# Scores of two pairs of heads issued as one run in every second step of a window attention

## The chip, the cores and the metric

The kernel runs on one core of a Trainium2 chip. The metric is the device time of one execution in microseconds, the median of several. Before the change three runs gave 798.02, 800.39 and 802.64 us; the median is 800.39 us.

A core has a matrix engine (TensorE, PE in the profile; its weight loads are listed as PEld), a vector engine (VectorE, DVE), a scalar engine (ScalarE, ACT) and GpSimd (POOL). Each works through its own queue in order; they wait for each other through semaphores. SyncE (SP) issues DMAs. TensorE writes to PSUM, which VectorE and ScalarE read.

## The reference

An attention over a window of 128 keys and 4 "sink" keys, then a Fourier mixing and a feed-forward network, in float32, for 4 batches of 768 positions, 8 heads of 64:

```python
scores = scale * np.matmul(q, k.transpose(0, 1, 3, 2))
keep = is_sink | in_window
scores = np.where(keep, scores, -1000000000.0)
a = np.exp(scores - np.max(scores, axis=-1, keepdims=True))
a = a / (np.sum(a, axis=-1, keepdims=True) + 1e-09)
x = np.matmul(a, v)                      # then heads side by side: (4, 768, 512)
u = x + np.real(np.fft.fft(np.fft.fft(x, axis=1), axis=2))
un = (u - mu) / np.sqrt(var + 1e-06)     # over the last axis
out = u + np.maximum(un @ w_ch1, 0.0) @ w_ch2
```

## The kernel before

**Blocks and steps.** The 768 positions of a batch are 6 blocks of 128 queries, so there are 24 blocks, numbered g. The 8 heads are 4 pairs, numbered hp. One *step* s is one pair of heads of one block: s = 4 g + hp, 96 steps in all, and k = s mod 4. A block needs its own 128 keys, the 128 of the block before it and the 4 sink keys.

**What is done for a pair** (names as they stand in the profile's rows):

- scores, on TensorE: queries times keys into a PSUM tile s. The queries and keys are split into a high and a low part (qs, and two rings of key blocks, ring), and three products of each head are added, so a pair is six matmuls (L723, 64 rows of the array each). The first block of a batch needs only its own keys, unsplit: two matmuls (L717). There are two PSUM tiles s, used in turn: the scores of step s can start when the softmax sums of step s - 2 have read theirs.
- merge, on VectorE (L730): the scores of the older keys are copied over those of the newer where the window wants them.
- soft1, on VectorE (L742): two instructions, one for each head, add the mask, take the extremum into mx and write to sm in SBUF.
- expo, on ScalarE (L748): the exponentials and their sums.
- For two pairs together: trans_p on TensorE (pt, L773, four transposes), copy_p on ScalarE (pta, L780), newer_p and older_p on GpSimd (ptl L789, pta L797, which separate newer from older keys), av on TensorE (xt, L811: the values, 128x64 pieces of the array).
- sink_p on GpSimd (sk, L759 and L760) and, once in a block, trans_sink on TensorE (pk, L829) and copy_sink on ScalarE (skt, L834). pk and pt use one and the same PSUM buffer.
- Once in a block: copy_x on ScalarE (xs, L816), turn_x on TensorE (x, L823 and L825), inverse on VectorE (L764, L765) and store_x on VectorE (L839: the product of x and 1/sum into u or us).
- Once in a block the next block's queries and keys are split: q_hi and k_hi on ScalarE (L686, L695), q_lo on VectorE or GpSimd (L691), k_lo on VectorE (L700, into ring).

**What sets the order.** The attention's instructions are recorded in the order of the text, with no scheduler, up to step 97 (`CUT`). In a step first the DMAs and the scores are recorded, then for each engine a list from `SCHEDULE[s >= 36][engine][k]`: names of the work above, and numbers and letters ("A", 0 to 3, "V", "G", "T") that stand for other events put at that step. `STEP_LAG` says how many steps after its scores a piece of a pair comes, `BLOCK_AT` the same for work done once in a block. With `lag(scores, s, 0)` step s records its own scores; with "merge" and "soft1" at a lag of 1, VectorE's list of step s holds the merge and sums of step s - 1.

**Fourier events.** Once four blocks of a batch are stored, the Fourier mixing of that batch is laid over the following steps: folds on VectorE and GpSimd (L351 to L367), then in TensorE's "T" events a first stage (za, zb, zr, L394) and a second one (a, b, dc, L421 and L442), whose results ScalarE and VectorE take out of PSUM (L399 to L409, L425 to L448). They use one PSUM bank of their own and at times the buffer of x.

**After step 97** a scheduler orders what is left: the tail of the last batches' Fourier work, the conversion of the FFN's weights on VectorE (cv, cw, L590 to L592), and the FFN of the first of seven groups. From the second group on the FFN is in the order of the text again; it is some 500 us of matmuls (h, L617, and o, L1147).

The lines that the change and the steps of the prediction touch are `STEP_LAG` (L71), the lists "V" of `SCHEDULE`, and `lag(scores, s, 0)` (L1000).

Of the kernel before, what the change touches and what calls it, by code (L numbers as in the profile page):

```python
# [67 lines left out]
POOL_LO = (1, 2, 3), ()  # L68
PHASE = 36

STEP_LAG = {"merge": 1, "soft1": 1, "expo": 2, "sink_p": 2, "trans_p": 3, "copy_p": 4, "newer_p": 5, "older_p": 5, "av": 7}  # L71
BLOCK_AT = {
    "copy_x": 11,
    "copy_sink": 8,
# [24 lines left out]
            ["copy_x", "A", "copy_p", "copy_sink", "expo", "q_hi", "k_hi", "mid_hi", "sink_hi"],  # L99
        ],  # L100
        "V": [
            ["merge", "inverse", "store_x", "q_lo", "k_lo", "sink_lo", "V", "soft1", 3, 0, "mid_lo", 1, 2],
            [3, "merge", 1, "V", "mid_lo", "soft1", "inverse", "store_x", "q_lo", "k_lo", 0, "sink_lo", 2],
            ["sink_lo", 0, "merge", 3, 1, "V", 2, "soft1", "store_x", "inverse", "k_lo", "mid_lo", "q_lo"],
            ["merge", "inverse", 0, "soft1", "k_lo", "V", 3, "store_x", "q_lo", "mid_lo", "sink_lo", 2, 1],
        ],
        "G": [
            ["q_lo_g", "mid_lo_g", "newer_p", "G", "older_p", "k_lo_g", "sink_p"],
# [16 lines left out]
            ["expo", "copy_x", "copy_p", "copy_sink", "A", "q_hi", "k_hi", "mid_hi", "sink_hi"],  # L125
        ],
        "V": [
            ["merge", "inverse", "store_x", "q_lo", "k_lo", "sink_lo", "soft1", 3, 1, 0, "V", 2, "mid_lo"],
            [2, "merge", 0, "sink_lo", 3, 1, "V", "soft1", "inverse", "q_lo", "store_x", "mid_lo", "k_lo"],
            ["sink_lo", "q_lo", 0, "merge", "soft1", 3, "V", 2, 1, "store_x", "inverse", "k_lo", "mid_lo"],  # L130
            ["merge", 1, "inverse", 3, 2, "soft1", "store_x", "q_lo", "V", 0, "k_lo", "mid_lo", "sink_lo"],
        ],
        "G": [
            ["q_lo_g", "mid_lo_g", "newer_p", "k_lo_g", "G", "older_p", "sink_p"],
# [81 lines left out]
def kernel(  # L216
# [15 lines left out]
    V, A, G, T = nc.vector, nc.scalar, nc.gpsimd, nc.tensor  # L232
# [37 lines left out]
    def run(general):  # L270
        tag = "g" if general else ""
        with ExitStack() as p1:
# [11 lines left out]
            def run_ev(s, eng):  # L284
                for fn in ev.pop((s, eng), ()):
                    fn()
# [346 lines left out]
            def window_attention(fourier, load_constants):  # L633
                with ExitStack() as pa:
# [207 lines left out]
                    def lag(fn, s, d):  # L842
                        if 0 <= s - d < len(steps):
                            fn(*steps[s - d])

                    last = len(steps) + 14
                    with ExitStack() as man:
# [131 lines left out]
                        s = 0  # L979
                        extra.append(lambda name: ps_t.tile([P, 512], F32, tag="x", name=name)  # L980
                                     if s % NP in X_AT and not X_NOT[0] <= s <= X_NOT[1] and s < len(steps) - 2 else None)
                        while s < last:
# [14 lines left out]
                                if g % NB == 2:  # L997
                                    load_v(kb(g) + 1)
                            run_ev(s, "S")
                            lag(scores, s, 0)  # L1000
                            if s == 0:
                                for (a, b, e), hi, lo in ((K0_AT, lambda: k_hi(kb(0)), lambda: k_lo(kb(0), V)),
                                                          (Q1_AT, lambda: q_hi(1), lambda: q_lo(1, V)),
# [365 lines left out]
```

## Time and profile before

| | us |
|---|---|
| median of 3 runs | 800.39 |
| the profiled execution | 802.72 |
| its span, first to last instruction | 800.9 |
| TensorE busy in it (95%) | 764.3 |
| VectorE busy (60%) | 479.8 |
| ScalarE busy (33%) | 263.2 |
| GpSimd busy (26%) | 205.1 |

The span and the busy times are of one profiled execution, 2.3 us above the median. A row of the timeline reads: start and length in us, engine, line, operation, output<-inputs, the part of the array (128\*64: rows by columns) and the shape, how many instructions are merged into it (x6), and in brackets how long the engine stood idle before it and what ended that. Matmuls are pipelined: one of them takes about 0.3 us from start to end, but the next starts long before that, so the place that a piece holds on TensorE is read from its start to the next piece's start. A row of busy time by stretch reads: the stretch, its length, then for each engine the us it was busy and (x) its instructions, the granted clock of TensorE (1.00 is full speed), the share of the DMA engines and GB/s.

### The profile page before, as it was taken

The page shows a single profiled execution, that of the slowest core. Times are in us where ns is not written, and L with a number is a line of the kernel's source. Part 1 is how long each engine was busy: PE and PEld are TensorE (multiplying, and loading weights), DVE is VectorE, ACT ScalarE, POOL GpSimd, SP SyncE. Part 2 cuts the span into 40 slices and gives each one's busy share as a digit, 9 for nine tenths or more (in the row PEclk, how much of TensorE's full clock was granted, in tenths as well). Part 3 has the DMA queues.
Part 4 walks back from the last instruction along what each step waited for, and adds up shares of the span by engine and source line. Part 5 has one row for each costly group of instructions (what it writes and reads, how often), then busy time and mean ns, then how long its engine had stood idle before and what let it go on. Part 6 is the DMA issues. An engine that isn't in the chain of part 4 may idle for free.

```text
span 800.9 us, 12364 instructions
## 1 busy us (share of the span) xinstructions
PE 764.3 (95%) x4539; PEld 631.8 (79%) x4539; DVE 479.8 (60%) x1387; ACT 263.2 (33%) x752; POOL 205.1 (26%) x298
## 2 busy tenths in 40 slices
PE   7988997998999899999999999999999999999995
PEld 5766886876778788889888888888888888888895
DVE  7989579899899679853256714663356515511211
ACT  6887586676642223312111111111111110110110
POOL 3568479579673335500000000000000000000000
PEclk9997999999999899999999999999999999999998
DMA  8652331324523446420010002000200001000100
GB/s 291 232 169 70 122 122 55 111 68 148 162 78 105 132 134 204 136 106 1 12 42 1 1 0 106 1 1 0 79 1 0 1 1 52 1 1 0 53 1 32
DMA packets 19926, 56.73 MB, mean 71 GB/s; under 512 B 2412, under 2 KB 2540, under 8 KB 19472
## 3 DMA queue, kind: packets, MB, share of 16 engines
q1 hardware_dynamic: 19568, 52.09, 19.6%
q0 software_dynamic: 288, 3.76, 1.1%
q8 instruction: 38, 0.62, 0.3%
q14 instruction: 32, 0.26, 0.1%
HBM read 46.39 MB, written 9.45 MB: 70 GB/s over the span
## 4 chain that ended last, share of the span: by engine, by line
PE 81%; DVE 11%; ACT 3%; issue 2%; POOL 1%; DMA 1%; SPq 0%; ACTq 0%; POOLq 0%; DVEq 0%
PE o L1147 32%; PE h L617 32%; PE xt L811 5%; PE s L723 3%; PE pt L773 2%; PE za L394 2%; DVE cv L591 1%; DVE sm L742 1%; PE a L421 1%; ACT sm L748 1%; PE zb L394 1%; DVE cv L590 1%; ACT pta L780 1%; PE b L442 1%; DVE s L730 1%
## 5 line engine op out<-in xcount | busy, mean ns | idle before, releaser
L1147 PE MATMUL o<-w,h 128*128 128x512 f32 x876 | 217.2, 395 | 0.0
L1140 DVE SCALAR_TENSOR_TENSOR h<-h,h 128x512 fp32r<-128x512 f32 (+1 forms) x107 | 65.4, 611 | 247.7 <-ACT h L1135 247.5
L1147 PEld LDWEIGHTS o<-w,h 128*128 128x128 f32 x876 | 164.3, 190 | 34.7
L1135 ACT ACTIVATE h<-h 128x512 fp32r<-128x512 f32 (+1 forms) x107 | 57.2, 535 | 365.7 <-PE h L617 365.7
L617 PE MATMUL h<-un_slots,w 128*128 128x512 f32 (+1 forms) x576 | 123.4, 363 | 0.0
L617 PEld LDWEIGHTS h<-un_slots,w 128*128 128x128 f32 x576 | 99.8, 188 | 18.1
L617 PE MATMUL h<-un_last,w 128*128 128x512 f32 (+1 forms) x432 | 88.6, 354 | 0.0
L617 PEld LDWEIGHTS h<-un_last,w 128*128 128x128 f32 x432 | 72.8, 189 | 12.4
L748 ACT ACTIVATE sm<-sm,mx 128x132 f32<-128x132 f32 x192 | 76.1, 400 | 12.0 <-DVE mx L742 11.8
L1171 DVE STREAM_TRANSPOSE unf<-un 32x128 f32<-32x128 f32 x224 | 67.7, 302 | 3.2
L723 PE MATMUL s<-ring,qs 64*128 64x260 f32 x480 | 53.0, 328 | 11.2 <-DVE mx L742 7.2
L723 PEld LDWEIGHTS s<-ring,qs 64*128 64x128 f32 x480 | 35.9, 195 | 26.5 <-issue 13.6
L742 DVE CUSTOM_DVE_ANT_0 sm<-s,mask 128x132 f32<-128x132 f32 x192 | 47.5, 284 | 2.2 <-PE pt L773 0.3
L606 POOL TENSOR_TENSOR w<-cv,w 128x512 fp32r<-128x512 f32 x25 | 34.0, 1359 | 32.0 <-ACT w L605 32.0
L811 PE MATMUL xt<-ptl,ldv 128*64 128x128 f32 x384 | 40.5, 295 | 0.0
L748 ACT ACTIVATION_READ_ACCUMULATOR sm<-sm,mx 128x1 f32 x192 | 36.7, 191 | 0.0
L1147 PE MATMUL o<-ring,h 128*128 128x512 f32 x144 | 35.5, 392 | 0.0
L789 POOL TENSOR_SCALAR_AFFINE_SELECT ptl<-pta 128x512 f32<-128x512 f32 x48 | 33.9, 706 | 6.1 <-ACT pta L780 6.0
L730 DVE COPY_PREDICATED s<-older,s 128x256 f32<-128x256 uint8 x80 | 33.4, 418 | 1.9 <-PE s L723 1.7
L780 ACT COPY pta<-pt 128x512 f32<-128x512 f32 x48 | 28.0, 583 | 18.8 <-PE pt L773 18.0
L773 PE MATMUL pt<-ident,sm 128*128 128x128 f32 x192 | 33.5, 301 | 0.0
L811 PE MATMUL xt<-pta,ldv 128*64 128x128 f32 x320 | 32.6, 282 | 0.0
(204 smaller groups left out, 1124.9 us busy)
## 6 DMA issues: line engine op xcount, KB each, us to landing
raw<-in_moe_w_ch_dram SPq DMA_DIRECT2D x32, 512.0 KB, 3.8
ld<-in_qk_dram SPq DMA_DIRECT2D x23, 524.0 KB, 3.8
ldv<-in_v_dram SPq DMA_DIRECT2D x28, 256.0 KB, 2.8
out_dram<-u SPq DMA_DIRECT2D x24, 256.0 KB, 2.0
cst<-in_dft_dram POOLq DMA_DIRECT2D x1, 3348.0 KB, 15.5
ud<-us SPq DMA_DIRECT2D x12, 256.0 KB, 2.0
u<-ud SPq DMA_DIRECT2D x2, 1024.0 KB
ldk<-in_k_mid_dram SPq DMA_DIRECT2D x4, 268.0 KB, 5.1
```

Of the source, the lines that this page charges most:

```text
L617: T.matmul(ps[:, :tb], a[:, cs], x[:, :, cc, :], start=n == 0, stop=n == 3 * NCC - 1)
L723: T.matmul(ps[:, j, :P + W], a[D * j:D * j + D, hp, :], keys(r, g, 2 * hp + j), start=i == 0, stop=i == 2)
L730: V.copy_predicated(ps[:, :, P + NS:P + W], older[qi > 2], ps[:, :, 0:P])
L742: V.tensor_tensor_reduce(sm[:, h % 4], ps[:, j, P:P + W], mask[min(qi, 3)], -SCALE, 3.0e38, ALU.add, ALU.min, accum_out=mx[:, 0, h:h + 1])
L748: A.activation(sm[:, h % 4], sm[:, h % 4], AF.Exp, bias=mx[:, 0, h:h + 1], scale=-1.0, accum_out=mx[:, 1, h:h + 1])
L773: T.transpose(ps[:, j], sm[:, j, NS:], ident)
L780: A.copy(a, st.pop(("pt", g, hp // 2)))
L811: T.matmul(ps[D * j:D * j + D, p, :], st["v", kb(g) - i][:, h, :], a[:, h % 4, :], start=i == 0, stop=i == n - 1)
L1135: A.activation(h[0], ps[:, :tb], AF.Relu)
L1140: V.scalar_tensor_tensor(h[1], ps[:, :tb], 0.0, f32(h[0]), op0=ALU.max, op1=ALU.subtract)
L1147: T.matmul(po[i], a[:, ts_], x, start=f == 0 and n == 0, stop=f == NF - 1 and n == 2)
L1171: V.transpose(unf[32 * q:32 * q + 32, :, r], un[r].rearrange("p (c q j) -> p c q j", c=NCC, q=4)[:, :, q])
```

## The change

Every second step records the scores of two steps, its own and those of the next, one right behind the other; the other steps record none. The merge and the softmax sums come at a lag of 0 instead of 1: in an even step they stand at the end of VectorE's list, in an odd step at its head, so that those of two pairs follow each other. In the lists of k = 3 k_lo is moved up to stand right behind them. The lists of the other engines are as before.

```diff
-STEP_LAG = {"merge": 1, "soft1": 1, "expo": 2, "sink_p": 2, "trans_p": 3, "copy_p": 4, "newer_p": 5, "older_p": 5, "av": 7}
+STEP_LAG = {"merge": 0, "soft1": 0, "expo": 2, "sink_p": 2, "trans_p": 3, "copy_p": 4, "newer_p": 5, "older_p": 5, "av": 7}
...
         "V": [
-            ["merge", "inverse", "store_x", "q_lo", "k_lo", "sink_lo", "V", "soft1", 3, 0, "mid_lo", 1, 2],
-            [3, "merge", 1, "V", "mid_lo", "soft1", "inverse", "store_x", "q_lo", "k_lo", 0, "sink_lo", 2],
...
-            ["merge", "inverse", 0, "soft1", "k_lo", "V", 3, "store_x", "q_lo", "mid_lo", "sink_lo", 2, 1],
+            ["inverse", "store_x", "q_lo", "k_lo", "sink_lo", "V", 3, 0, "mid_lo", 1, 2, "merge", "soft1"],
+            ["merge", "soft1", 3, 1, "V", "mid_lo", "inverse", "store_x", "q_lo", "k_lo", 0, "sink_lo", 2],
...
+            ["merge", "soft1", "k_lo", "inverse", 0, "V", 3, "store_x", "q_lo", "mid_lo", "sink_lo", 2, 1],
...
                             run_ev(s, "S")
-                            lag(scores, s, 0)
+                            if s % 2 == 0:
+
+                                lag(scores, s, 0)
+                                lag(scores, s, -1)
```

**TensorE, block 10, from its first scores on; the first Fourier stage (za) runs over these steps.** s_10_0, s_10_1 and s_10_2 are the scores of the block's first three pairs. Before, from pt, which stands behind the values of that step, to the second half of za:

```order
L773 MATMUL pt_9_1_1337<-ident_63,sm_9_0_1233 128x128 x4
L394 MATMUL za0_0_1342<-cst_87,gh_0_867 128x386 x2
L394 MATMUL za0_0_1342<-cst_87,gl_0_868 128x386
L394 MATMUL za0_0_1342<-cst_87,gh_0_867 128x386 x2
L823 MATMUL x_7_1348<-ident_63,xs_7_1288 128x128 x4
L825 MATMUL x_7_1348<-vs_1_822,skt_7_1182 128x512
L723 MATMUL s_10_1_1354<-ring0_79,qs0_10_1186 128x260 x2
L723 MATMUL s_10_1_1354<-ring0_79,qs1_10_1187 128x260 x2
L723 MATMUL s_10_1_1354<-ring1_80,qs0_10_1186 128x260 x2
L394 MATMUL za0_0_1342<-cst_87,gl_0_868 128x386
```

and now, from the second pair's scores on, which stand ahead of the values and of pt:

```order
L723 MATMUL s_10_1_1317<-ring0_79,qs0_10_1196 128x260 x2
L723 MATMUL s_10_1_1317<-ring0_79,qs1_10_1197 128x260 x2
L723 MATMUL s_10_1_1317<-ring1_80,qs0_10_1196 128x260 x2
L811 MATMUL xt_8_1340<-ptl_8_1_1271,ldv_9_1152 64x128 x2
L811 MATMUL xt_8_1340<-pta_8_1_1232,ldv_8_1033 64x128 x2
L811 MATMUL xt_8_1340<-ptl_8_1_1271,ldv_9_1152 64x128 x2
L811 MATMUL xt_8_1340<-pta_8_1_1232,ldv_8_1033 64x128 x2
L773 MATMUL pt_9_1_1349<-ident_63,sm_9_0_1203 128x128 x4
L394 MATMUL za0_0_1354<-cst_87,gh_0_869 128x386 x2
L394 MATMUL za0_0_1354<-cst_87,gl_0_870 128x386
L394 MATMUL za0_0_1354<-cst_87,gh_0_869 128x386 x2
L823 MATMUL x_7_1360<-ident_63,xs_7_1292 128x128 x4
```

The six matmuls of s_10_1 moved from behind x to ahead of the values xt; the two halves of za now have only x between them.

**TensorE, block 5, where no Fourier product runs: the end of the block.** Before:

```order
L773 MATMUL pt_4_3_781<-ident_63,sm_4_2_687 128x128 x4
L723 MATMUL s_5_3_788<-ring0_79,qs0_5_584 128x260 x2
L723 MATMUL s_5_3_788<-ring0_79,qs1_5_585 128x260 x2
L723 MATMUL s_5_3_788<-ring1_80,qs0_5_584 128x260 x2
L829 MATMUL pk_4_811<-ident_r_104,sk_4_692 128x128
```

and now:

```order
L773 MATMUL pt_4_3_792<-ident_63,sm_4_2_661 128x128 x4
L829 MATMUL pk_4_814<-ident_r_104,sk_4_695 128x128
L717 MATMUL s_6_0_818<-ld_6_574 128x132 x2
L717 MATMUL s_6_1_821<-ld_6_574 128x132 x2
L811 MATMUL xt_4_840<-ptl_4_1_781,ldv_5_680 64x128 x2
```

The scores s_5_3 no longer stand between pt and pk; the next block's first two scores follow pk.

**VectorE, the same block 5, second half.** s_2 and s_3 are the third and fourth pair's scores; ring_80 is the low part of the keys. Before:

```order
L730 COPY_PREDICATED s_2_757<-older_122,s_2_757 128x2x128
L764 TENSOR_SCALAR mx_630<-mx_630 128x8
L765 RECIPROCAL mx_630<-mx_630 128x8
L742 ISA sm_2_804,mx_751<-s_2_757,mask_126 128x132
L742 ISA mx_751 128x1
L742 ISA sm_2_804,mx_751<-s_2_757,mask_126 128x132
L742 ISA mx_751 128x1
L700 TENSOR_TENSOR ring_80<-ld_571,ring_79 128x4x132
L730 COPY_PREDICATED s_3_788<-older_122,s_3_788 128x2x128
```

and now:

```order
L730 COPY_PREDICATED s_3_767<-older_122,s_3_767 128x2x128
L742 ISA sm_2_778,mx_724<-s_3_767,mask_126 128x132
L742 ISA mx_724 128x1
L742 ISA sm_2_778,mx_724<-s_3_767,mask_126 128x132
L742 ISA mx_724 128x1
L700 TENSOR_TENSOR ring_80<-ld_574,ring_79 128x4x132
L764 TENSOR_SCALAR mx_601<-mx_601 128x8
L765 RECIPROCAL mx_601<-mx_601 128x8
```

The ring's low part stood behind the sums of the third pair and ahead of the fourth's; now it stands behind the fourth's, and the reciprocal behind it.

More of the change, by code (lines that the diff above doesn't have):

```diff
@@ L101 @@
         "V": [
-            ["merge", "inverse", "store_x", "q_lo", "k_lo", "sink_lo", "V", "soft1", 3, 0, "mid_lo", 1, 2],
-            [3, "merge", 1, "V", "mid_lo", "soft1", "inverse", "store_x", "q_lo", "k_lo", 0, "sink_lo", 2],
-            ["sink_lo", 0, "merge", 3, 1, "V", 2, "soft1", "store_x", "inverse", "k_lo", "mid_lo", "q_lo"],
-            ["merge", "inverse", 0, "soft1", "k_lo", "V", 3, "store_x", "q_lo", "mid_lo", "sink_lo", 2, 1],
+            ["inverse", "store_x", "q_lo", "k_lo", "sink_lo", "V", 3, 0, "mid_lo", 1, 2, "merge", "soft1"],
+            ["merge", "soft1", 3, 1, "V", "mid_lo", "inverse", "store_x", "q_lo", "k_lo", 0, "sink_lo", 2],
+            ["sink_lo", 0, 3, 1, "V", 2, "store_x", "inverse", "k_lo", "mid_lo", "q_lo", "merge", "soft1"],
+            ["merge", "soft1", "k_lo", "inverse", 0, "V", 3, "store_x", "q_lo", "mid_lo", "sink_lo", 2, 1],
         ],
@@ L127 @@
         "V": [
[L128 to L131, printed above, removed]
+            ["inverse", "store_x", "q_lo", "k_lo", "sink_lo", 3, 1, 0, "V", 2, "mid_lo", "merge", "soft1"],
+            ["merge", "soft1", 2, 0, "sink_lo", 3, 1, "V", "inverse", "q_lo", "store_x", "mid_lo", "k_lo"],
+            ["sink_lo", "q_lo", 0, 3, "V", 2, 1, "store_x", "inverse", "k_lo", "mid_lo", "merge", "soft1"],
+            ["merge", "soft1", "k_lo", 1, "inverse", 3, 2, "store_x", "q_lo", "V", 0, "mid_lo", "sink_lo"],
         ],
```

## The prediction

> **What bounds the kernel now.** I read the forty slices first, then the busy time by stretch, then the order of TensorE's work inside a stretch, and last the waits.
>
> ```profile
> PE   7988997998999899999999999999999999999995
> DVE  7989579899899679853256714663356515511211
> PEclk9997999999999899999999999999999999999998
> ```
>
> Each digit is the busy share of 20 us. From the fourteenth slice on, TensorE is full to the end and VectorE mostly is not: this is the FFN, and the change does not touch it. The scores that the change moves are all issued in the first eleven slices. There both engines read 7 to 9, so neither bounds it alone, and the stretches have to be taken apart.
>
> ```profile
> core 0: us, PE busy (x) PEld busy (x) DVE busy (x) ACT busy (x) POOL busy (x), PEclk, DMA share, GB/s
> 20.00:60.00 40.00, 36.13 (x381) 28.07 (x379) 34.93 (x158) 35.22 (x129) 24.11 (x47) 0.96 0.58 201
> 60.00:80.00 20.00, 17.08 (x145) 13.17 (x146) 19.18 (x67) 15.39 (x55) 16.79 (x26) 0.78 0.25 68
> 80.00:120.00 40.00, 40.00 (x360) 32.83 (x357) 26.70 (x104) 28.34 (x98) 22.93 (x39) 0.98 0.38 123
> 120.00:140.00 20.00, 15.91 (x145) 12.34 (x144) 18.21 (x61) 13.53 (x48) 19.48 (x29) 0.91 0.17 55
> 140.00:160.00 20.00, 20.00 (x178) 16.37 (x178) 17.57 (x73) 13.66 (x48) 11.10 (x20) 1.00 0.33 111
> 160.00:220.00 60.00, 54.26 (x482) 43.45 (x480) 56.08 (x197) 42.76 (x144) 46.46 (x69) 0.97 0.40 126
> 220.00:260.00 40.00, 37.71 (x246) 32.16 (x245) 39.85 (x72) 14.97 (x36) 22.88 (x22) 1.00 0.28 93
> ```
>
> Three kinds of stretch can be told apart. From 80 to 120 and from 140 to 160 TensorE has no gap, and VectorE stands for 13.3 and 2.4 us: less TensorE work is worth its full size there. From 60 to 80, 120 to 140 and 160 to 220 VectorE is busy 91 to 96%, with 0.8 + 1.8 + 3.9 = 6.5 us free in all, and from 120 to 140 GpSimd is at 97%: TensorE's savings are mostly hidden there. From 20 to 60 nobody is full and the engines hand work to each other in a ring. After 220 VectorE is full (39.85 of 40), with the conversion of the FFN's weights: whatever the attention gains or loses on VectorE is handed on from there to the FFN, and so to the end.
>
> **The change part by part.** No arithmetic is removed. The order of TensorE shows 86 separate runs of scores before and 48 after: 38 runs are now joined to the one ahead. What a joined run saves is read where both forms stand in the trace.
>
> ```profile
> 28.10 1.01 PE L723 MATMUL s<-ring,qs 64*128 64x260 f32 x12
> 29.04 0.44 PE L811 MATMUL xt<-ptl,ldv 128*64 128x128 f32 x4
> ...
> 30.06 0.66 PE L773 MATMUL pt<-ident,sm 128*128 128x128 f32 x4
> 30.76 0.63 PE L723 MATMUL s<-ring,qs 64*128 64x260 f32 x6
> 31.71 0.25 PE L829 MATMUL pk<-ident_r,sk 128*128 128x128 f32 x1 [0.32 <-ACT pta L780]
> 31.89 0.82 PE L723 MATMUL s<-ring,qs 64*128 64x260 f32 x6
> 32.64 0.44 PE L811 MATMUL xt<-ptl,ldv 128*64 128x128 f32 x4
> ...
> 34.51 0.48 PE L825 MATMUL x<-vs,skt 128*128 128x512 f32 x1
> 34.92 0.99 PE L723 MATMUL s<-ring,qs 64*128 64x260 f32 x12
> 35.85 0.33 PE L811 MATMUL xt<-ptl,ldv 128*64 128x128 f32 x2
> ```
>
> ```profile
> 93.28 0.63 PE L723 MATMUL s<-ring,qs 64*128 64x260 f32 x6
> 93.84 0.45 PE L394 MATMUL zr<-cst,gl 128*128 128x386 f32 x1
> ...
> 94.48 0.34 PE L394 MATMUL zr<-cst,gl 128*128 128x386 f32 x1
> 94.66 0.34 PE L394 MATMUL zr<-cst_row,sph 128*128 128x386 f32 x1
> 94.92 0.64 PE L723 MATMUL s<-ring,qs 64*128 64x260 f32 x6
> 95.49 0.44 PE L811 MATMUL xt<-ptl,ldv 128*64 128x128 f32 x4
> ```
>
> The shapes 64\*128, 128\*128 and 128\*64 are three ways in which the array is divided. A run of six scores holds TensorE from 93.28 to 93.84, that is 0.56 us; a run of twelve from 34.92 to 35.85, 0.93 us. The second six of a joined run therefore cost 0.37, and 0.19 is saved behind them. Ahead of a run there is a loss too: two Fourier products follow each other after 0.18 us (94.48 to 94.66), but the scores come 0.26 after (94.66 to 94.92), 0.08 more. Behind the turned values they come after 0.41 us (34.51 to 34.92) for 512 columns, which at 0.18 for 386 would be 0.24: 0.17 more. I take 0.13 between the two. A joined run saves about 0.32 us of TensorE, with 0.27 and 0.37 as ends, and 38 of them some 12 us. How much of it counts depends on the stretch:
>
> - **80 to 120 and 140 to 160.** Sixteen and eight single runs of scores start there, so eight and four are joined away: 8 x 0.32 = 2.6 and 4 x 0.32 = 1.3 us, at full value since TensorE has no gap. Gain **3.9**.
> - **The VectorE-bound stretches.** The 6.5 us in which VectorE stands there bound the gain from above, and nothing from below. TensorE is ahead of VectorE there, so I stay near the lower end: gain **0.6**.
> - **20 to 60.** Here no Fourier product runs, and the order before already had the second and third scores of a block joined (the x12 at 28.10). The change pairs first with second and third with fourth, so it also takes the single six at 30.76 out from between pt and pk. Those two share one PSUM buffer: pk waits until ScalarE has copied pt, and at 31.71 it still waited 0.32 us for this with the scores in between. It will start no earlier without them; that run was free. The other single run, 0.75 us long (31.89 to 32.64), becomes a run of 0.93. So a block takes 0.18 us more, or 0.37 if the single run counts as 0.56. About six blocks (one takes 34.92 - 28.10 = 6.82) make 1.1 to 2.2: loss **1.6**. Below nothing I go to a gain of 1, which the next point could bring.
> - **VectorE's order.** Merge and softmax sums keep their number. In an odd step those of two pairs now stand together ahead of the normalized store (us or u, L839), which waits for the turned values x:
>
> ```profile
> DVE us L839 <- PE x L825: 8.4, 4, 3.1
> DVE u L839 <- PE x L825: 5.1, 6, 1.6
> PE pk L829 <- ACT pta L780: 6.1, 10, 1.8
> PE s L723 <- DVE ring L700: 3.8, 3, 1.9
> 8.00 0.69 DVE L691 TENSOR_TENSOR qs<-ld,qs 128x512 fp32r<-128x512 f32 x1 [1.24 <-ACT qs L686]
> ```
>
>   The columns are us in total, times, and the longest. The 13.5 us of waits for x shrink wherever the second pair fills them, but where TensorE is the bound this only moves VectorE's idle time, so it is given no value beyond the 3.9. Against it, the low part of the next block's keys (ring, L700) now stands behind the sums of the fourth pair instead of the third, and the next two pairs of scores wait for it, with the values and transposes queued behind them. Both are costed at nothing net; either end is below. At the start, the second pair's sums move ahead of qs L691 and fill part of its 1.24 us wait: gain **0.7**, ends 0 and 1.24.
> - **Hidden edits.** ScalarE's and GpSimd's orders are unchanged through the attention, and the softmax sums come earlier or at the same place as seen from ScalarE, so the exponentials lose nothing. After step 97 a scheduler places the conversions anew among the Fourier tail. VectorE is full there and its work is the same, so I cost this at nothing, with 2 us either way, an estimate: one conversion more or less ahead of what TensorE waits for, which takes 0.67 us at one place and 1.71 at another:
>
> ```profile
> 230.91 0.67 DVE L592 SCALAR_TENSOR_TENSOR cv<-raw,cv 128x512 int32<-128x512 int32 x1
> 258.14 1.71 DVE L591 SCALAR_TENSOR_TENSOR cv<-raw,cv 128x512 int32<-128x512 int32 x1
> ```
>
> The sum is -3.9 - 0.6 + 1.6 - 0.7 = **-3.6 us**. Against the profiled execution (802.72 us, of which 800.9 is the span) this gives 799.1; the median of the runs shown is 800.39, so the forecast for the median is **796.8 us**.
>
> **The rivals.**
>
> *More than the sum.* TensorE's late pieces cost VectorE more than their own size. This row follows a stretch in which the granted clock was 0.78 (60 to 80 above):
>
> ```profile
> 83.21 0.69 DVE L839 TENSOR_TENSOR us<-x,mx 128x512 f32<-128x512 f32 x1 [3.12 <-PE x L825]
> ```
>
> If the shorter queue removes this wait of 3.1 us and half of the 6.5 us, the time is 796.8 - 3.1 - 2.7 = about 791. For it: x stands behind fewer switches. Against it: the slow clock came from waits that remain.
>
> *Hidden.* VectorE and GpSimd set the pace even where TensorE reads full, because busy time of TensorE includes its pipeline. Then only the start and the loss remain, +0.9: 801.3. For it: 95% busy is modelled. Against it: VectorE's 13.3 free us from 80 to 120.
>
> *Slower: the scores were the cover.* Between two TensorE pieces that depend on each other through another engine (pt and pk; two Fourier pieces that share one PSUM bank) stood a run of scores; now the pieces of an even and an odd step touch, and TensorE waits in the open. Each place costs up to the 0.56 us of the run. Ten waits of pk are in the trace already; with all of them longer by 0.56, and an estimated ten places more in the Fourier second stage, it costs 20 x 0.56 = 11.2 us in place of the 1.6 above; less the gains of 5.2 that is +6.0: 806.4. It decides from about ten such places on the path (5.2 / 0.56), and shows beyond the border from some sixteen. For it: the row of pk. Against it: where Fourier products run in the first stage, one stands between pt and pk.
>
> *The clock.* In this trace the clock halves after little TensorE work:
>
> ```profile
> 126.00:128.00 2.00, 0.83 (x9) 0.43 (x5) 1.93 (x8) 2.00 (x9) 1.92 (x6) 1.00 0.00 0
> 128.00:130.00 2.00, 0.72 (x4) 0.49 (x6) 1.94 (x6) 0.51 (x1) 2.00 (x2) 0.81 0.00 0
> 130.00:132.00 2.00, 2.00 (x18) 1.67 (x17) 2.00 (x5) 0.00 (x0) 2.00 (x3) 0.50 0.02 4
> 132.00:134.00 2.00, 2.00 (x17) 1.76 (x17) 2.00 (x7) 1.17 (x4) 2.00 (x3) 0.84 0.00 0
> ```
>
> After 4 us with 1.55 us of work the clock reads 0.81, 0.50 and 0.84; (0.19 + 0.50 + 0.16) x 2 = 1.7 us of TensorE time are lost. Less work in the same time makes such pauses likelier where VectorE bounds. Four more of them on the path cost 6.8 us: 796.8 + 6.8 = 803.6. The Trainium skill speaks against this change here ("TensorE: Matmul & The Clock Gate", Part 1): the clock falls to half after an idle window of about 3.4 us and needs a busy one to return. The rows above agree with the falling and with about the length.
>
> **How the numbers follow.** A difference under 0.5% (4.0 us, so between 796.4 and 804.4) cannot be told from no change. The forecast gets 0.44, with its own range 793 to 801; it lies almost on the border, so 0.18 of it is faster and 0.26 the same. More than the sum gets 0.21, all faster; hidden 0.10, the same; the lost cover 0.18, slower; the clock 0.07, of which 0.03 the same and 0.04 slower. Together: faster 0.39, same 0.39, slower 0.22. With every unknown at its better end (start 1.24, 20 to 60 a gain of 1, 12 joined runs at 0.37, and most of the 6.5) the time is near 788; the lost cover gives 806.4, which I round up to 807. That many of these meet at once is less than 2 in 10.
>
> **What would show it.** Runs of scores should read x12 with 0.93 us to the next piece. From 80 to 120 the same work should end about 2.6 us sooner, with VectorE's waits for x smaller. In the blocks before 60 us, pk should wait 0.9 us instead of 0.3, and a block last 7.0 us instead of 6.8. The last softmax sum, in this row of before, should start about 3.6 us sooner:
>
> ```profile
> 221.60 0.28 DVE L742 CUSTOM_DVE_ANT_0 sm<-s,mask 128x132 f32<-128x132 f32 x1
> ```
>
> The forecast is wrong if the pause after the low part of the keys grows on TensorE in every block, if the clock falls below 0.9 in more than five slices, or if the conversions after 220 us leave VectorE idle.

## The result

| | before | after |
|---|---|---|
| median | 800.39 us (7 runs, 798.02 to 802.88) | 805.97 us (7 runs, 803.61 to 807.43) |
| the profiled execution | 802.72 us, span 800.9 | 807.05 us, span 805.3 |
| mean granted TensorE clock in it | 0.979 | 0.972 |
| VectorE busy in it | 479.8 us | 486.9 us |

The ratio is 1.0065 with a 95% interval of 1.0042 to 1.0088: the change makes the kernel slower by 5.6 us. The forecast was 796.8, on the other side; the time is inside the range, near its upper end.

The forty slices of the profile after:

```profile
PE   7887997987988999999999999999999999999995
DVE  7989689999999868954147614564356515511211
PEclk9998997999999999999999999999999999999999
```

VectorE's nines reach from the seventh slice to the thirteenth without a break, where before an 8 stood in the eighth and in the eleventh. The busy time by stretch of the profile after, in the columns of before:

```profile
20.00:60.00 40.00, 34.87 (x383) 27.40 (x380) 35.13 (x150) 33.18 (x123) 22.91 (x44) 0.96 0.52 183
80.00:120.00 40.00, 39.55 (x377) 34.17 (x378) 28.71 (x110) 30.61 (x106) 23.72 (x43) 0.96 0.43 137
120.00:140.00 20.00, 15.27 (x129) 12.09 (x126) 18.99 (x59) 12.71 (x46) 18.43 (x27) 0.82 0.14 43
160.00:220.00 60.00, 51.63 (x466) 43.57 (x465) 56.10 (x196) 40.81 (x142) 44.57 (x67) 0.91 0.40 125
220.00:260.00 40.00, 35.41 (x236) 29.44 (x235) 39.23 (x76) 15.92 (x40) 22.43 (x24) 0.91 0.21 67
```

From 80 to 120 us TensorE got through more (377 instructions against 360) and is no longer quite full, as it would be if the joined runs save time there. From 160 to 220 TensorE falls from 54.3 to 51.6 us busy, VectorE stays at 56.1: TensorE now stands more, VectorE as little as before, and yet the work comes later.

The waits up to 224 us that the prediction spoke of, after (us in total, times, the longest):

```profile
PE pk L829 <- ACT pta L780: 13.3, 12, 2.6
PE s L723 <- DVE ring L700: 6.4, 8, 2.4
DVE us L839 <- PE x L825: 5.9, 3, 2.3
DVE u L839 <- PE x L825: 3.1, 6, 1.4
```

pk waits 13.3 us for ScalarE instead of 6.1, the scores 6.4 for the keys instead of 3.8; VectorE's waits for x fell from 13.5 to 9.0.

Where the time goes is read best from one instruction that stands in every block: pk. Its start in blocks 0 to 23, against the same block of before (us; plus is later), from the timelines of this kernel and of the experiments below, with the end of the span. Each row is one profiled execution, and these lie from 2.6 us under their kernel's median (merges_first) to 2.3 above it (before), so the last column is not the difference of the medians:

| pk of block | 0 | 4 | 7 | 12 | 17 | 20 | 22 | span's end |
|---|---|---|---|---|---|---|---|---|
| before, at | 18.09 | 45.07 | 68.04 | 117.65 | 167.11 | 197.75 | 219.89 | 800.9 |
| after | -0.42 | 3.01 | 3.38 | 0.33 | 1.22 | 3.89 | 8.70 | 4.4 |
| low_part_first | -1.16 | 2.35 | 2.81 | -1.84 | -0.84 | 2.44 | 7.17 | 1.1 |
| pk_behind | 2.35 | 3.45 | 4.98 | 0.07 | 3.01 | 5.59 | 7.27 | 2.1 |
| joined_late | 0.05 | -0.56 | 0.08 | -5.27 | -4.35 | -1.68 | 3.40 | -1.3 |
| joined_early | 0.11 | 2.68 | 3.03 | 1.31 | 0.39 | 2.09 | 2.05 | 1.3 |
| merges_first | -0.81 | 1.02 | 1.09 | -4.74 | -5.37 | -3.47 | -3.61 | -6.7 |
| before_adjacent | -0.39 | 4.24 | 5.03 | 4.05 | 3.64 | 6.43 | 6.84 | 7.9 |
| merges_pk | -0.38 | 2.22 | 2.27 | -3.80 | -4.49 | -2.58 | -1.57 | -4.4 |

After: 3.4 us are lost up to block 4, 3.1 won between block 7 and 12, and 8.4 lost between block 12 and 22, mostly in the stretches that VectorE bounds. Some 4 us come back in the tail: in the trace after, VectorE has done four weight conversions more (L590 to L592) by the store of block 22, 5.3 us of work that before stood behind it. So most of the 8.4 is work done in another order, and not lost.

### The profile page after: what moved, and what is told of

Its sections match the earlier page's. It is cut to its first block, busy times and chain, and to the rows that moved or that the text cites. A ratio compares the mean times of both kernels' runs of the same rounds, so it can differ in the third digit from the quotient of the medians.

```text
span 805.3 us, 12369 instructions
## 1 busy us (share of the span) xinstructions
PE 762.4 (95%) x4539; PEld 636.6 (79%) x4539; DVE 486.9 (60%) x1387; ACT 263.1 (33%) x752; POOL 205.0 (25%) x298
## 4 chain that ended last, share of the span: by engine, by line
PE 79%; DVE 10%; POOL 4%; ACT 3%; issue 2%; DMA 0%; SPq 0%; DVEq 0%; POOLq 0%; ACTq 0%
PE o L1150 33%; PE h L617 32%; PE xt L811 3%; PE s L723 3%; PE za L394 2%; PE pt L773 2%; DVE sm L742 1%; ACT sm L748 1%; PE zb L394 1%; DVE ring L700 1%; DVE s L730 1%; DVE f L351 1%; PE zr L394 1%; ACT pta L780 1%; DVE cv L591 1%
## 5 line engine op out<-in xcount | busy, mean ns | idle before, releaser
L1150 PEld LDWEIGHTS o<-w,h 128*128 128x128 f32 x876 | 162.8, 188 | 34.1
L723 PE MATMUL s<-ring,qs 64*128 64x260 f32 x480 | 46.4, 322 | 8.1 <-DVE ring L700 6.4
L811 PE MATMUL xt<-ptl,ldv 128*64 128x128 f32 x384 | 43.3, 310 | 0.0
L789 POOL TENSOR_SCALAR_AFFINE_SELECT ptl<-pta 128x512 f32<-128x512 f32 x48 | 33.1, 691 | 13.7 <-ACT pta L780 10.5
L811 PE MATMUL xt<-pta,ldv 128*64 128x128 f32 x320 | 34.4, 293 | 0.0
L730 DVE COPY_PREDICATED s<-older,s 128x256 f32<-128x256 uint8 x80 | 33.6, 420 | 0.0
```

What stands on the lines that cost most here:

```text
L723: T.matmul(ps[:, j, :P + W], a[D * j:D * j + D, hp, :], keys(r, g, 2 * hp + j), start=i == 0, stop=i == 2)
L730: V.copy_predicated(ps[:, :, P + NS:P + W], older[qi > 2], ps[:, :, 0:P])
L811: T.matmul(ps[D * j:D * j + D, p, :], st["v", kb(g) - i][:, h, :], a[:, h % 4, :], start=i == 0, stop=i == n - 1)
L1150: T.matmul(po[i], a[:, ts_], x, start=f == 0 and n == 0, stop=f == NF - 1 and n == 2)
```

## The experiments

Four theories stood in turn. **A**: the low part of the keys (L700), now behind the fourth pair's sums, holds up the next scores. **B**: the scores were the cover between pt and pk. **C**: the granted clock of TensorE, which in the trace of before had read 0.50 for two microseconds after a pause. **D**, formed after the first four runs: VectorE's own time, because the merge now stands directly ahead of the sum that reads it. All times of the experiments are compared with runs of before on the same chip; these had medians of 800.9 to 801.4 us.

### Theories A and B: low_part_first and pk_behind

low_part_first moves one name in both lists of k = 3:

```diff
-            ["merge", "soft1", "k_lo", "inverse", 0, ...
+            ["k_lo", "merge", "soft1", "inverse", 0, ...
```

> The change as it is, but in the last step of each block VectorE makes the low part of the next block's keys (L700) ahead of the softmax sums of the fourth pair, where it stood by neighbours before the change (behind the sums of the third pair). Theory A (the low part came too late: the next block's scores wait for it): TensorE's waits of scores for ring fall from 6.4 us in 8 places to the 3.8 us in 3 places of before or less, the 2.43 us wait near 125 us goes, each block from 20 to 55 us gets 0.3 to 0.4 us shorter, and the time is about 803 us (3 less than the changed kernel's 806). Theory B (the loss is the lost cover between pt and pk): pk's waits for ScalarE stay at 13 us in 12 places and the time stays at 806 within 1. Theory C (the clock): waits for ring go, but the time follows the number of slices below full clock after 160 us, whichever way.

Measured: 804.57 us, ratio 1.0060 (1.0037 to 1.0084), not to be told from the change itself. Of TensorE's waits up to 224 us:

```profile
PE pk L829 <- ACT pta L780: 15.0, 12, 3.1
PE s L723 <- DVE mx L742: 8.2, 15, 1.9
PE s L723 <- DVE ring L700: 3.5, 1, 3.5
```

The waits for the keys did fall as theory A says, from eight to one, but their time came back as waits for the sums (mx, 8.2 against 1.6), which VectorE now makes after the keys. Up to block 4 the loss is the same, 3.5 us (-1.16 to 2.35). Whatever is put first, VectorE is late. The mean clock in this execution was 0.987, and the kernel took 803.8 us; executions of before with that clock took 797.2 to 799.3. So theory C alone does not carry the loss.

pk_behind issues pk after the joined scores (its name is taken out of the lists "T"):

```diff
-    "trans_sink": 7,
+    "trans_sink": 8,
...
+                            if k == 0 and 0 <= g - 2 < NQ:
+                                trans_sink(g - 2)
```

> The change as it is, but pk, the turned sink probabilities, is issued behind the next two runs of scores instead of ahead of them, so that a run of twelve matmuls again stands between pt and pk, which share one PSUM buffer. Theory B (lost cover): the waits of pk for ScalarE's copy fall from 13.3 us to under 4, the blocks from 20 to 55 us go back to the lengths of before (0.75 us shorter each), and the time is about 802.5 us. Theory A (the low part of the keys came too late): the scores now start sooner and wait for ring by as much longer as pk waited before them, 806 within 1. A price that can show: ScalarE's copy of pk comes 0.9 us later with the exponentials behind it.

Measured: 804.73 us, ratio 1.0059 (1.0036 to 1.0082), again not to be told from the change. TensorE's longest waits up to 224 us:

```profile
PE s L723 <- DVE ring L700: 10.9, 12, 2.6
PE s L723 <- DVE mx L742: 7.4, 10, 1.2
```

pk no longer waits for ScalarE at all; the scores wait for the keys and the sums in its place. Up to block 4 it loses 1.1 us instead of 3.4, but only because it has lost 2.35 already at block 0, where pk stands behind scores that are not ready. Theory B foresaw 802.5; the waits went where theory A said, and A had failed in its own run. The price that was foreseen came too: ScalarE waits 22.4 us for pk, where in the change it waits 3.9, so this run alone does not rule out theory B; merges_pk below covers pk with 5.1 us of such waits. The keys and the sums are both VectorE's work: in these waits its lateness shows.

### Where it is lost: joined_late and joined_early

These use the changed order only from step 36 on, or only up to step 35 (`JOIN = -1, 36`; the sums at the seam are kept whole):

```diff
+JOIN = 36, 1000
...
+                            joined = JOIN[0] <= s < JOIN[1]
...
-                                for op in SCHEDULE[s >= PHASE][e][k]:
+                                for op in SCHEDULE[s >= PHASE]["VJ" if e == "V" and joined else e][k]:
```

> The changed order from step 36 on alone (from about 89 us); up to there the kernel before's order. If the orders of single blocks explain the loss (theories A and B, which cost 0.75 us a block only where no Fourier products run), block 9 starts where it does before, 80 to 120 us still gains 2 to 3 us, and the time is 800 to 803. If the loss comes after 160 us by the clock or by the tail (theory C), this kernel keeps most of it: 803.5 to 806.

> The changed order up to step 35 alone (to about 89 us); from there the kernel before's order. Theories A and B: blocks 1 to 5 lose 0.75 us each, some 3.4 us at 70 us, of which 1.9 was left at block 9 in the changed kernel; 802 to 804. Theory C: the early part costs little at the end, since later waits swallow it; 800 to 801.5.

Measured: joined_late 804.20 us, ratio 1.0051 (1.0030 to 1.0072); joined_early 803.45, ratio 1.0034 (1.0020 to 1.0048). They cost 3.3 and 2.5 us, together about what the whole costs (0.9 of the 3.3 lies outside joined_late's span). joined_late came out on the side of theory C, and joined_early within the range of A and B: no theory had both. The row of joined_late in the table is the telling one: 5.3 us ahead of before at block 12, and by block 22 behind it by 3.4. From the timelines I then added up, at the normalized store of each block, VectorE's idle time and its busy time so far. At block 22 VectorE had stood 2.7 us less than before in the changed kernel (4.8 less in joined_late, 6.2 less in low_part_first), and had been busy 10.7 us longer (7.5 and 12.6). In all three, 5.3 of this are the four conversions done earlier; the rest is no other work, and over the whole run VectorE is busy 7.1 us longer (486.9 against 479.8) with the same instructions. So VectorE's waits were really shorter, and it needed more time.

### Theory D: what stands behind a merge

Start, length, instruction: VectorE's timeline of before, at two merges (L730).

```profile
168.54 0.41 DVE L730 COPY_PREDICATED s<-older,s 128x256 f32<-128x256 uint8 x1
168.87 0.91 DVE L526 SCALAR_TENSOR_TENSOR stat<-stat 128x4 f32<-128x4 f32 x1
...
175.24 0.42 DVE L730 COPY_PREDICATED s<-older,s 128x256 f32<-128x256 uint8 x1
175.70 0.30 DVE L742 CUSTOM_DVE_ANT_0 sm<-s,mask 128x132 f32<-128x132 f32 x1
```

And of the changed kernel:

```profile
42.63 0.41 DVE L730 COPY_PREDICATED s<-older,s 128x256 f32<-128x256 uint8 x1
43.18 0.29 DVE L742 CUSTOM_DVE_ANT_0 sm<-s,mask 128x132 f32<-128x132 f32 x1
...
43.62 0.42 DVE L730 COPY_PREDICATED s<-older,s 128x256 f32<-128x256 uint8 x1
44.08 0.30 DVE L742 CUSTOM_DVE_ANT_0 sm<-s,mask 128x132 f32<-128x132 f32 x1
```

Behind a merge an operation that does not read it mostly starts after 0.33 us, while the merge's row still runs. The sum that reads it starts after 0.46 us, just past the end of the row, or in some places after 0.55. Before, the lists put a normalized store, a fold or a reciprocal between the two wherever one was due; the change writes "merge", "soft1" side by side. Counted over all 80 merges (long waits that begin behind a merge, of 0.6 us or more, are taken as 0.33):

| | merges directly ahead of their sum | all 80, start to next start | VectorE busy | ratio to before |
|---|---|---|---|---|
| before | 33 | 31.2 us | 479.8 us | 1 |
| after | 70 (24 of them 0.55 or more) | 37.7 | 486.9 | 1.0065 |
| joined_late | 51 | 34.7 | 483.6 | 1.0051 |
| joined_early | 52 | 34.3 | 479.7 | 1.0034 |
| merges_first | none (40 stand ahead of the other pair's sum) | 27.2 | 478.3 | 0.9978 |
| before_adjacent | 71 | 37.4 | 488.7 | 1.0134 |

The Trainium skill bears on this twice. "Perfetto Trace Analysis", DVE / Act Engine Instruction, says that a row ends when the memory has acknowledged the last write and that only then the semaphore goes out; the rows agree, since the reader starts 0.04 us behind the merge's end (43.62 + 0.42 to 44.08) and an operation that does not depend on it 0.08 ahead (168.54 + 0.41 to 168.87). "VectorE: DVE Perf Modes", The DRAIN you can't avoid, says of eight copies in a row that a semaphore after each of them "costs nothing extra here". No run here has such a chain; for a sum that must wait for its merge the measured price is 0.13 us and more, and for this pair that decides.

merges_first keeps the change and only moves the merges of both pairs ahead of both pairs' sums:

```diff
-            ["inverse", "store_x", ..., 1, 2, "merge", "soft1"],
-            ["merge", "soft1", 3, 1, "V", ...
+            ["inverse", "store_x", ..., 1, 2, "merge", "merge2", "soft1", "soft2"],
+            [3, 1, "V", ...
```

> The change as it is, but VectorE merges the scores of both pairs (L730) ahead of both pairs' softmax sums (L742), so that no merge stands directly ahead of the sum that reads it. Theory D (VectorE's own time): in the trace of before 33 merges stand directly ahead of their sum and take 0.46 us to the next start, 47 have another operation behind them and take 0.33; in the changed kernel 70 stand directly ahead, and 24 of those take 0.55 or more. That is 70 x 0.49 + 10 x 0.33 = 37.8 us against 33 x 0.47 + 47 x 0.33 = 31.0, or 6.8 us more of VectorE ahead of its last sum. With the merges together all 80 should take about 0.33, VectorE reaches the normalized store of block 22 with about 10 us less of its own time than in the changed kernel, and the time is 796 to 801. Theories A, B and C (the low part of the keys, the cover of pt and pk, the clock): the time stays at 804 to 807.

before_adjacent keeps the kernel before and only moves each merge down to its sum:

```diff
-            ["merge", "inverse", "store_x", "q_lo", "k_lo", "sink_lo", "V", "soft1", 3, ...
+            ["inverse", "store_x", "q_lo", "k_lo", "sink_lo", "V", "merge", "soft1", 3, ...
```

> The kernel before with one edit: each merge is moved down to stand directly ahead of the sums of its pair; the sums and all scores stay where they are. Theory D: 38 more merges stand directly ahead of their sum at 0.13 to 0.16 us more each, 5 to 6 us of VectorE; the time rises to 803 to 806, as in the changed kernel, with no run of scores joined. Theories A, B and C: 800 to 801.5, since TensorE's order is that of before.

Measured: merges_first 798.60 us, ratio 0.9978 (0.9957 to 0.9999): 7.4 us under the changed kernel, and just under before. before_adjacent 810.54 us, ratio 1.0134 (1.0109 to 1.0160), slower than the change itself, though TensorE's order is that of before. Both go the way of theory D, the second by more than it foresaw (803 to 806). The order of VectorE in merges_first differs from the changed kernel's in the place of the merges and, late in the attention, of a few small instructions of the normalization. Its store of block 22 comes 10.8 us sooner than the changed kernel's; by then VectorE has been busy as long as in the kernel before (within 0.1 us), with three conversions more (3.9 us) done. In before_adjacent that store comes 7.7 us later than before, VectorE has been busy 7.9 us longer and has stood no longer: the loss is its own time. By the table its 38 more merges are worth 6.2 us (37.4 - 31.2), and its conversions up to there took 2.1 us longer. In merges_first's timeline two merges share a row:

```profile
43.38 0.75 DVE L730 COPY_PREDICATED s<-older,s 128x256 f32<-128x256 uint8 x2
44.04 0.29 DVE L742 CUSTOM_DVE_ANT_0 sm<-s,mask 128x132 f32<-128x132 f32 x1
```

Two merges, 0.66 us to the first sum, which reads the one that is 0.33 older. In 37 of 40 places this sum starts less than 0.4 us behind the merge ahead of it, so the 0.13 us do not come from the kind of operation behind the merge: they come where it reads that merge. The groups of the sums up to 232 us (busy us, mean ns, then the idle time ahead of them). Of before:

```profile
L742 DVE CUSTOM_DVE_ANT_0 sm<-s,mask 128x132 f32<-128x132 f32 x192 | 47.5, 284 | 2.2 <-PE pt L773 0.3 <-DVE mask L900 0.2
```

After:

```profile
L742 DVE CUSTOM_DVE_ANT_0 sm<-s,mask 128x132 f32<-128x132 f32 x192 | 48.5, 292 | 6.8 <-PE s L717 1.6 <-DVE s L730 0.2 <-POOL ptl L789 0.2
```

Of merges_first:

```profile
L742 DVE CUSTOM_DVE_ANT_0 sm<-s,mask 128x132 f32<-128x132 f32 x192 | 44.8, 287 | 2.5 <-PE s L717 2.0 <-DVE s L730 0.2 <-DVE mask L900 0.2
```

Of before_adjacent:

```profile
L742 DVE CUSTOM_DVE_ANT_0 sm<-s,mask 128x132 f32<-128x132 f32 x192 | 48.8, 292 | 5.3 <-DVE mask L900 0.2
```

The cost is hard to see here: 5.3 and 6.8 us of idle time ahead of the sums where 2.2 and 2.5 stand in the two faster kernels, most of it put down to nothing, and the rest where rows no longer overlap. Only the distance from start to start shows it.

### The two halves of the change alone: scores_alone and sums_alone

scores_alone joins the runs of scores and leaves VectorE its old order; since both score buffers must be free, the scores are recorded behind VectorE's list of the step. sums_alone takes VectorE's new order and leaves the scores single.

```diff
 scores_alone
+                                if e == "T" and s % 2 == 0:
+                                    lag(scores, s, 0)
+                                    lag(scores, s, -1)
 sums_alone
-                            if s % 2 == 0:
-                                lag(scores, s, 0)
-                                lag(scores, s, -1)
+                            lag(scores, s, 0)
```

> The joined runs of scores with VectorE's order of before (merge and sums one step later and apart; the scores of two pairs are issued once the sums of the pair ahead are emitted). Theory D: VectorE's time per block is that of before, TensorE keeps what the joining saves from 80 to 160 us (some 4 us), and the time is 797 to 801. Theory B (joining itself uncovers pt and pk): the blocks up to 60 us are as long as in the changed kernel and the time is 803 or more. A price that would muddle it: with two pairs in hand and both score buffers held a step longer, TensorE may wait for the sums at each joined run, which would show as waits of s for mx.

> The changed order of VectorE with each pair's scores in their old place in TensorE's order: no run is joined. Theory D: 70 merges stand directly ahead of their sum as in the changed kernel, VectorE's busy time is that of the changed kernel (486.9 us) or near it, and what the joined runs save is gone: slower than the changed kernel by 1 to 4 us, so 807 to 810. Theory B (the loss comes from the joined runs, which take the cover from pt and pk): faster than the changed kernel, 799 to 802, with pk's waits back at 6 us. If the even pair's sums, which now stand at the end of the step in which their scores are issued, only moved earlier, nothing: 800 to 801.

Measured: scores_alone 831.53 us, ratio 1.0387 (1.0351 to 1.0422); sums_alone 827.07, ratio 1.0319 (1.0292 to 1.0347). Neither was foreseen, and neither tells the theories apart: each half has a stall of its own that the other half takes away. VectorE's longest waits up to 224 us in scores_alone:

```profile
DVE s L730 <- PE s L723: 11.4, 8, 2.7
DVE u L839 <- PE x L825: 11.2, 10, 2.5
```

and the longest in sums_alone:

```profile
DVE s L730 <- PE s L723: 34.1, 19, 3.8
```

With sums_alone the odd pair's sums stand at the head of the step in which their scores are only issued, and VectorE waits 34.1 us for them. With scores_alone the scores wait for all earlier sums and VectorE then for the scores. In the change the joined run makes the odd pair's scores ready a step ahead, and its sums may follow at once.

### What is left over: merges_low, merges_pk, merges_late

Three variations on merges_first: the low part of the keys between the third and the fourth pair's sums (merges_low); pk behind the joined scores in blocks 1 to 6 (merges_pk); the order of before up to step 35 (merges_late).

```diff
 merges_low, k = 2
-            [..., "k_lo", ..., "merge", "merge2", "soft1", "soft2"],
+            [..., "merge", "merge2", "soft1", "k_lo", "soft2"],
 merges_pk
+                            if k == 0 and 1 <= g - 2 <= 6:
+                                trans_sink(g - 2)
 merges_late
+JOIN = 36, 1000
```

> As merges_first, and the low part of the next block's keys (L700) is made between the third and the fourth pair's sums in place of behind the fourth's. Theory A and D together: the waits of scores for ring fall below the changed kernel's 6.4 us in 8 places, and the time is 1 to 1.5 us under merges_first, as low_part_first was 1.4 under the changed kernel: 795 to 800. D alone: as merges_first within 1 us.

> merges_first, and in blocks 1 to 6 alone (no Fourier products there) pk is issued behind the next two runs of scores, so that these stand between pt and pk. Theory B as the rest of the loss up to 60 us: with the merges apart, blocks 1 to 4 still lose 1.0 us against before while pk waits about 0.8 us in each; with the cover back they lose nothing, and the time is 1 us under merges_first: 797 to 798. If the scores then wait for the keys instead, nothing: 798.6 within 1.

> merges_first from step 36 on; up to there the order of before, singles and all. If the stretch up to 60 us only loses by the new order (1.2 us at block 6 in merges_first), this is 1 to 2 us faster: 796.5 to 798. If what VectorE saves on its merges ahead of step 36 counts there too (in merges_first block 8 stands 0.9 us ahead of before, after a loss of 1.2 at block 6), it is 798.6 to 800.

Measured: merges_low 800.44 us, ratio 0.9995 (0.9980 to 1.0010); merges_pk 798.76, ratio 0.9981 (0.9962 to 1.0001); merges_late 799.53, ratio 0.9976 (0.9960 to 0.9992). None can be told from merges_first by its interval. merges_low missed both of its ranges; merges_pk and merges_late came out where no gain was foreseen. The waits of pk from 20 to 60 us. Before:

```profile
PE pk L829 <- ACT pta L780: 3.5, 6, 1.8
```

After:

```profile
PE pk L829 <- ACT pta L780: 4.3, 5, 1.0
```

In merges_first:

```profile
PE pk L829 <- ACT pta L780: 4.3, 5, 1.0
```

In merges_pk:

```profile
PE pk L829 <- ACT pta L780: 0.2, 1, 0.2
```

After and merges_first wait the same 4.3 us for pk, yet between block 0 and 4 one loses 3.4 us and the other 1.8; and merges_pk, where pk hardly waits, loses 2.6. The cover of pk was worth little, and taking it away was not what made the blocks longer. What costs the 1.8 us that merges_first still loses there is open; merges_late, with the order of before in these blocks, loses none (0.42 us late at block 0, 0.38 at block 4).

## Why the prediction was wrong

The step that failed is the point **VectorE's order**: "Merge and softmax sums keep their number", and the two effects of the new order that it names are "costed at nothing net". What a merge costs when it stands right ahead of its sum is not among them. The number stayed, the time did not. With merge and sum side by side, 37 more merges wait for their own write, 6.5 us of VectorE (37.7 - 31.2) that the sum of terms has at zero. before_adjacent, which moves the merges and nothing else, costs 9.3 us; merges_first, which undoes this and keeps the joined runs, wins back 7.4. Added to the forecast of -3.6, the 6.5 would have given +2.9; the change measured +5.6.

For the remaining 2.7 no cause is shown. VectorE's busy time grew by 7.1 us. Counting each row only where no earlier row still runs, 4.4 of this stand at the sums (2.8 because they no longer start while the merge's row runs, 1.6 because their own rows are longer, 292 ns against 284); the other 2.6 are spread over many groups, each up or down by 1.7 at most. The total does not follow the merges alone: joined_early has 52 merges ahead of their sums and the busy time of before. The granted clock can hold part of the 2.7. In the executions of before in the experiments a clock of 0.979 went with 801.2 to 803.6 us and one of 0.987 to 0.989 with 797.2 to 799.3, some 4 us for 0.009. The seven of the changed kernel had 0.972 to 0.980, 0.975 in the mean, where before had 0.983: by that slope, an estimate, some 3 us. At the same clock of 0.980 the changed kernel took 804.6, before 802.0 to 802.2 and merges_first 797.7 to 800.3. With the merges apart the clock was back at 0.981, but whether the late merges lowered it was not tried.

Point by point:

- **Joined runs, 80 to 120 and 140 to 160, gain 3.9.** A joined run holds TensorE for 0.93 us, as forecast:

```profile
86.97 1.00 PE L723 MATMUL s<-ring,qs 64*128 64x260 f32 x12
87.90 0.44 PE L811 MATMUL xt<-ptl,ldv 128*64 128x128 f32 x4
```

  Between block 7 and 12 the changed kernel gains 3.1 us, joined_late 5.4 and merges_first 5.8, against the 2.6 forecast up to 120 us; what they gain beyond the joined runs was not taken apart. The 1.3 from 140 to 160 is not there: from block 14 (137 us) to block 16 (158 us) pk loses 1.0 us.
- **The VectorE-bound stretches, gain 0.6.** Here the failed step is paid: from block 12 to 22 the changed kernel loses 8.4 us, of which 5.3 are the conversions done earlier; merges_first gets 1.1 later, with 3.9 of conversions done earlier. The forecast said that TensorE's savings are hidden there; it did not ask whether VectorE's work stays the same size.
- **20 to 60, loss 1.6.** It lost 3.4 between block 0 and 4. With the merges apart it loses 1.8: in size the term came out, and VectorE's merges came on top. But that is luck, since its reason was not the cover of pk, as merges_pk shows, and the real one is open. "pk waits 0.9 instead of 0.3" did come true:

```profile
40.58 0.25 PE L829 MATMUL pk<-ident_r,sk 128*128 128x128 f32 x1 [0.82 <-ACT pta L780]
...
41.69 0.39 PE L723 MATMUL s<-ring,qs 64*128 64x260 f32 x2 [0.42 <-DVE ring L700]
```

  and the block lasted 7.50 us (pk at 40.58, the next at 48.08) instead of 7.0: a sign that comes true can still name the wrong cause.
- **Low part of the keys, nothing net.** Right: low_part_first and merges_low are no faster than the kernels they were made from.
- **The start, gain 0.7.** pk of block 0 starts 0.42 us sooner, but 0.11 later in joined_early and 0.81 sooner in merges_first, so a gain of this size is not shown.
- **The tail, nothing within 2.** Some 4 us came back there, because conversions had been done earlier. The last softmax sum came 5.7 us later in place of 3.6 sooner:

```profile
227.31 0.28 DVE L742 CUSTOM_DVE_ANT_0 sm<-s,mask 128x132 f32<-128x132 f32 x1
```

Of the rivals, "the scores were the cover" named 806.4 and hit the time with the wrong mechanism: covering pk again gained nothing. Without pk_behind, merges_pk and merges_first the number alone would have passed for a proof. "The clock" foresaw slower slices; the clock did fall, and may hold part of the rest as said above, but at an equal clock the changed kernel is still slower, and low_part_first was slower than before at 0.987. "More than the sum" asked whether the shorter queue takes away VectorE's waits. In part it does: VectorE's waits for x fell from 13.5 to 9.0 us, and at block 22 it had stood 2.7 us less. That merges_first is 2.6 us under before does not show what this is worth, because merges_first also parts the 33 merges that stood ahead of their sums before, 4.0 us of VectorE (31.2 - 27.2).

One reading of the forty slices was off: "both engines read 7 to 9" does not hold for VectorE's fifth slice, which reads 5, and TensorE reads 8 in the fourteenth and is full from the fifteenth. The sum does not use either; it goes by the busy time by stretch. The upper end of what a joined run saves adds up to 0.36, not 0.37.

What stays open: why 24 of the 70 merges read 0.55 us and not 0.46 (in the changed kernel all 24 stand at a block's first or third pair, whose sums open a new buffer; the buffer alone does not cost it, since in merges_first the same sums start less than 0.4 us behind the other pair's merge in 37 of 40 places), and how much of merges_first's gain is to be had without joining the scores, by parting the 33 merges of before alone.

## What to carry to other kernels

When an edit moves instructions on the engine that bounds a stretch, price each pair of neighbours anew, from start to next start: in these traces an operation that did not read the merge ahead of it overlapped the merge's tail, and one that read it did not. Write producers of independent data side by side and their consumers behind them, two and two, instead of pair by pair. And when a wait grows after a change, cover it again before calling it the cause: here the waits of pk for ScalarE rose from 6.1 to 13.3 us, and they are still 12.3 in merges_first, which is not slower than before.

## What the runs showed that was not expected

A merge of 128x256 on VectorE costs 0.46 us to the next start when the next operation reads it, in the changed kernel 0.55 or more in a third of these places, and mostly 0.33 with another operation behind it: 80 merges make 10.5 us between the best order measured (27.2) and the worst (37.7). The idle time shows under the reader as time that little explains (6.8 us ahead of 192 sums, of which 0.2 is put down to the merges).

And what a grown pause of TensorE costs cannot be read from the pause alone. In the changed kernel TensorE stood 2.43 us for the middle block's keys ahead of pk of block 13, and its clock read 0.50 from 126 to 132 us:

```profile
122.61 0.51 PE L723 MATMUL s<-ring,qs 64*128 64x260 f32 x4
125.56 0.94 PE L723 MATMUL s<-ring,qs 64*128 64x260 f32 x8 [2.43 <-DVE ring L700]
```

pk of blocks 12, 13 and 14 was 0.33, 2.70 and 0.84 us late, so 1.9 of the 2.4 us lost were back one block later. Between these two blocks the kernel before has a pause for keys of its own, and its clock reads 0.50 from 130 to 132 us:

```profile
129.28 0.59 PE L723 MATMUL s<-ring,qs 64*128 64x260 f32 x2 [1.93 <-DVE ring L700]
```
